# Moving one early input load to a second DMA queue in a transformer-block kernel

## The chip, the cores and the metric

The kernel runs on one core of one Trainium2 chip. The metric is the device time of one execution in microseconds (us). A profile comes from one further execution; its span (first to last instruction) is about 1.7 us shorter than that execution's time. All comparisons use runs classed as fast. A difference counts as "faster" or "slower" only beyond 2%.

## The reference

The input x has 2048 tokens of 640 numbers, in bf16. It is layer-normalised; then a linear-attention branch and a GELU branch are added to x.

```python
xn = layernorm(x)                                  # no learned scale
q, k, v = split(xn @ wqkv)                         # 32 heads of 20
phi = lambda t: where(t > 0, t + 1, exp(t)) + 1e-6
kv  = einsum("bhsd,bhse->bhde", phi(k), v)
z   = phi(k).sum(over s)
o   = (phi(q) @ kv) / (phi(q) @ z + 1e-6)
out = x + o @ wo + gelu(xn @ w1 + b1) @ w2 + b2
```

## The kernel before

The tokens come in 16 tiles of 128. "x0" to "x3" are the loads of tiles 0 to 3 (160 KB each). The K columns of wqkv come in two parts: part one is rows 0 to 383 (480 KB), part two the last 256 rows (320 KB). DMAs are issued from two queues: the sync queue and ScalarE's queue.

```python
def load_x(t0, t1, queue=nc.sync):
    queue.dma_start(out=x_all[:, t0:t1, :], in_=xv[:, t0:t1, :])

def load_wk(k0, k1):
    nc.scalar.dma_start(out=wqk[:, k0:k1, D : 2 * D], in_=wqkv_v[:, k0:k1, D : 2 * D])

load_x(0, 1)          # x0 .. x3, all on the sync queue
load_x(1, 2)
load_x(2, 3)
load_x(3, 4)
# ... later loads are issued further down
nc.vector.memset(eps_t[:], EPS)
nc.vector.memset(neg_half[:], -0.5)
nc.vector.memset(wqk[:, 0, D : D + TOK], 0.0)   # "gate": K part one must wait for it
load_wk(0, 3)         # K part one, ScalarE's queue
load_wk(3, NC)        # K part two
load_x(4, 8, nc.scalar)
```

The memset writes bytes that the K load overwrites, so the load may not be issued before it. It serves only to hold the load back. The compute that follows has this order; every engine keeps its own order of instructions:

```python
emit_warm(10)                       # TensorE: ten matmuls on constants
emit_stats(0); emit_center(0)       # VectorE: mean and variance of tile 0; tile 0 centred
emit_T_first(0, ...)                # TensorE transposes tile 0, ScalarE copies it out
emit_warm(1)
emit_stats(1)
emit_later_loads()                  # W1 and others, sync queue
emit_stats(2)
emit_rstd(0, 2)                     # ScalarE: 1/sqrt(var + eps)
emit_norm(1)                        # VectorE: tile 1 normalised
emit_Ka(0)                          # TensorE: K of tile 0, needs both K parts
emit_rstd(2, 3)
emit_T_first(1, ...)
emit_stats_half(3, 0)               # VectorE: first half of x3's statistics
emit_norm(2)                        # VectorE: tile 2 normalised, behind it
emit_stats_half(3, 1)
emit_Kb(0)                          # TensorE: the last 128 K columns of tile 0
emit_T(2, ...)                      # TensorE transposes tile 2
emit_Ka(1, 0, 3)
# ... K of tiles 1 to 3, then the GELU branch; TensorE is full from here on
```

Tile 2 is normalised behind an instruction that needs x3.

Of the kernel before, what the change touches and what calls it, by code (L numbers as in the profile page):

```python
# [15 lines left out]
def kernel(  # L16
# [12 lines left out]
    nc = tc.nc  # L29
# [4 lines left out]
    S, D = x2d.shape  # L34
# [6 lines left out]
    TOK = 512  # L41
# [34 lines left out]
    wqk = early.tile([P, NC, 2 * D], BF16, name="wqk", tag="early")  # L76
# [47 lines left out]
# [4 lines that stand above are left out]
        nc.scalar.dma_start(out=wqk[:, k0:k1, D : 2 * D], in_=wqkv_v[:, k0:k1, D : 2 * D])  # L128

    load_x(0, 1)  # L130
    load_x(1, 2)
    load_x(2, 3)
    load_x(3, 4)

# [8 lines left out]

    nc.vector.memset(eps_t[:], EPS)
    nc.vector.memset(neg_half[:], -0.5)
    nc.vector.memset(wqk[:, 0, D : D + TOK], 0.0)
    load_wk(0, 3)
    load_wk(3, NC)
    load_x(4, 8, nc.scalar)
# [1081 lines left out]
```

## Time and profile before

| | |
|---|---|
| time, median of the 20 runs beside the changed kernel | 197.07 us (196.64 to 197.34) |
| span in the trace | 195.4 us |
| TensorE busy | 188.8 us, 97% |
| TensorE's waits after its start | 1.2 + 0.4 + 0.2 us, all before 9.6 us |
| transpose of tile 2 | 9.60 us |

These lines are from the page of the kernel before: busy time by engine, the granted TensorE clock in tenths over 40 slices, and the chain that ended last, by engine. In all such lines PE is TensorE (PEld its weight loads), DVE is VectorE, ACT is ScalarE, POOL is GpSimd and SP the sync engine; a q after the name means that the engine's queue is issuing. L and a number is a line of the kernel.

```profile
...
PE 188.8 (97%) x1229; PEld 111.3 (57%) x1240; DVE 163.8 (84%) x393; ACT 89.8 (46%) x165; POOL 21.4 (11%) x54
...
PEclk9999999999999999999999999999999999999999
...
PE 93%; DMA 3%; issue 1%; DVE 1%; SPq 1%
...
```

TensorE bounds the kernel: it is busy 97% of the span at full clock (the mean granted clock is 1.0; a 9 stands for 90% or more), and 93% of the last chain is TensorE. A change elsewhere can help only where TensorE waits. The list of TensorE's waits (who waited, for whom, us in total, times, longest) of the kernel before:

```profile
...
PE bank_198 L242 <- DVE xn L229: 1.2, 1, 1.2
...
PE bank_170 L318 <- DMA wqk<-in_A_wqkv_dram: 0.4, 1, 0.4
PE bank_170 L318 <- ACT xnT L268: 0.2, 1, 0.2
```

L242 is the transpose of tile 2, L318 the K matmuls. Why is there a wait of 1.2 us for a VectorE result? The chain of waits over the first 12 us (start, duration, what):

```profile
...
2.19 6.48 DMA x_all<-in_A_x_dram
...
8.70 0.04 DVE stats L209
...
9.11 0.44 DVE xn L229
...
9.60 0.45 PE bank_198 L242 x5
...
```

After the issues on the sync queue (left out) comes one piece of 6.48 us: x3 travelling until 8.67 us. Then VectorE starts x3's first statistics half, normalises tile 2 at 9.11, and TensorE can transpose it at 9.60. The timeline of the same stretch (start, duration, engine, line, what; in brackets the idle time before it and what ended it) shows the issues and the landings:

```profile
...
0.81 1.82 SPq L125 DMA_DIRECT2D x_all<-in_A_x_dram  x4
...
0.99 0.27 DVE L146 MEMSET wqk<- 128x256 uint32 x1
...
1.29 0.96 ACTq L128 DMA_DIRECT2D wqk<-in_A_wqkv_dram  x2
...
3.13 0.89 DVE L209 BATCH_NORM_STATS2 stats<-x_all 128x6 f32<-128x320 bf16 x2 [1.87 <-DMA x_all<-in_A_x_dram]
...
6.13 0.89 DVE L209 BATCH_NORM_STATS2 stats<-x_all 128x6 f32<-128x320 bf16 x2 [0.40 <-DMA x_all<-in_A_x_dram]
...
8.70 0.50 DVE L209 BATCH_NORM_STATS2 stats<-x_all 128x6 f32<-128x320 bf16 x1 [1.12 <-DMA x_all<-in_A_x_dram]
...
```

The four x issues take 1.82 us, about 0.45 us each. The memset ends at 1.26 us and ScalarE issues K part one at 1.29. VectorE starts on x0 at 3.13, on x2 at 6.13 and on x3 at 8.70 us. The DMA view from 4.1 to 4.6 us (packets, MB, share of the 16 DMA engines' time; q1 is the sync queue, q10 ScalarE's) shows why x2 and x3 are late:

```profile
...
q10 hardware_dynamic: 153, 0.20, 106.0%
q1 hardware_dynamic: 1, 0.00, 0.1%
...
```

ScalarE's queue moves 153 packets of K part one, the sync queue a single packet, although x2 was issued at 1.72 us. The trace's records of landings give the order x0 3.11, x1 4.50, K part one 5.60, x2 6.11, K part two 7.06, x3 8.67 us. This is the order of issue over both queues. But x3 came 1.6 us after K part two, and its 160 KB need only some 0.4 us (an estimate, at the 390 GB/s seen from 4 to 5 us). The view from 7 to 8 us shows what slowed it:

```profile
...
q10 hardware_dynamic: 73, 0.37, 91.4%
q1 hardware_dynamic: 44, 0.04, 12.2%
...
```

ScalarE's queue was by then on x4 to x7 (640 KB, issued at 2.28 us, 0.1 us after x3). Its packets are of 5 KB and those of x3 of 1.3 KB, so x3 got 0.04 MB of that microsecond and x4 to x7 0.37. Behind K part two alone x3 would have landed near 7.5 us by the same estimate, and VectorE was free for it at 7.58. So by this estimate the load of x4 to x7 is part of the cause of the wait for x3. This is argued, not shown: no run held that load back alone.

The Trainium skill's page "DMA: Bandwidth & Descriptors", section "Queues, rings and completion order", says that each DMA engine takes turns between the queues that have work, packet by packet. Between 4.1 and 4.6 us this trace does not show such turns. Whether x2 already lay before the engines at 4.1 us is not shown.

### The profile page before, as it was taken

How to read it: one execution, taken by the hardware profiler on the slowest of the kernel's cores; microseconds unless marked ns; L12 is line 12 of the kernel's file. 1: busy time of each engine (PE TensorE's matmuls, PEld its weight loads, DVE VectorE, ACT ScalarE, POOL GpSimd, SP SyncE). 2: the span in 40 equal slices, each digit the busy share in tenths (PEclk: the TensorE clock that was granted, in tenths of full speed). 3: DMA queues.
4: the chain of work that ended last, by engine and by line, in shares of the span. 5: the costliest groups of instructions: out<-in, count | busy, mean ns of one | idle time of the engine just before them, and what ended most of it. 6: DMA issues, size and time to landing. Idle time of an engine off the chain costs nothing.

```text
span 195.4 us, 3334 instructions
## 1 busy us (share of the span) xinstructions
PE 188.8 (97%) x1229; PEld 111.3 (57%) x1240; DVE 163.8 (84%) x393; ACT 89.8 (46%) x165; POOL 21.4 (11%) x54
## 2 busy tenths in 40 slices
PE   8699999999999999999999999999999999999993
PEld 2364444544445454444445777767767777777772
DVE  4678988999699999597787999989999999777442
ACT  2459676559579678899795230050011010110100
POOL 1004071003219200001500100000000000000000
PEclk9999999999999999999999999999999999999999
DMA  5999446944144000000008875400201021010112
GB/s 173 388 285 393 176 91 140 352 150 89 38 151 105 0 0 2 0 0 3 0 0 205 307 240 164 129 3 2 70 0 60 7 70 47 22 67 3 67 56 78
DMA packets 24447, 20.19 MB, mean 103 GB/s; under 512 B 11120, under 2 KB 24048, under 8 KB 24432
## 3 DMA queue, kind: packets, MB, share of 16 engines
q1 hardware_dynamic: 23472, 18.36, 30.8%
q10 hardware_dynamic: 960, 1.64, 2.3%
q8 instruction: 9, 0.15, 0.3%
q14 instruction: 6, 0.05, 0.1%
HBM read 12.78 MB, written 5.24 MB: 92 GB/s over the span
## 4 chain that ended last, share of the span: by engine, by line
PE 93%; DMA 3%; issue 1%; DVE 1%; SPq 1%
DMA x_all<-in_A_x_dram 3%; PE bank_1274 L832 2%; PE bank_1283 L832 2%; PE bank_1210 L803 2%; PE bank_1557 L975 1%; PE bank_2113 L975 1%; PE bank_1435 L975 1%; PE bank_1945 L975 1%; PE bank_2029 L975 1%; PE bank_1861 L975 1%; PE bank_1772 L975 1%; PE bank_1683 L975 1%; PE bank_1399 L832 1%; PE bank_1387 L832 1%; PE bank_1511 L975 1%; PE bank_1581 L975 1%
## 5 line engine op out<-in xcount | busy, mean ns | idle before, releaser
L975 PEld LDWEIGHTS <-xn 128*128 128x128 f16 x198 | 19.0, 98 | 7.2
L493 PEld LDWEIGHTS <-w_91 128*128 128x128 bf16 x120 | 11.7, 98 | 13.9
L209 DVE BATCH_NORM_STATS2 stats<-x_all 128x6 f32<-128x320 bf16 x32 | 13.8, 469 | 3.4 <-DMA x_all<-in_A_x_dram 3.4
L481 PEld LDWEIGHTS <-wqk 128*128 128x128 bf16 x100 | 9.6, 98 | 11.1
L318 PEld LDWEIGHTS <-xnT 128*128 128x128 bf16 x80 | 7.2, 98 | 7.3 <-issue 0.7
L832 PEld LDWEIGHTS <-xn 128*128 128x128 bf16 (+1 forms) x80 | 7.8, 98 | 3.0
L229 DVE TENSOR_SCALAR xn<-x_all,mv,rstd 128x640 bf16<-128x640 bf16 x16 | 6.2, 436 | 3.7 <-POOL rstd L225 3.6
L890 DVE TENSOR_TENSOR pqT<-pqT,xnT 128x256 bf16<-128x256 bf16 (+1 forms) x30 | 8.5, 328 | 0.0
L636 PEld LDWEIGHTS <-w_91 128*128 128x128 bf16 (+1 forms) x48 | 4.6, 98 | 5.6 <-issue 0.3
L328 PEld LDWEIGHTS <-xnT 128*128 128x128 bf16 x80 | 5.8, 98 | 3.5
L990 PEld LDWEIGHTS <-Sq 128*128 128x128 f16 x66 | 6.3, 98 | 2.5 <-DVE Sq L881 0.2
L420 DVE TENSOR_TENSOR x_all<-x_all,b2b 128x640 bf16<-128x640 bf16 x16 | 7.0, 479 | 0.0
L172 POOL TENSOR_SCALAR_AFFINE_SELECT emask<-emask 128x160 int8<-128x160 int8 (+3 forms) x20 | 6.7, 346 | 0.9
L279 DVE TENSOR_SCALAR pqT<-pqT 128x512 bf16<-128x512 bf16 x20 | 5.7, 285 | 0.6 <-ACT pqT L276 0.6
L990 PEld LDWEIGHTS <-pqT 128*128 128x128 bf16 x50 | 4.8, 98 | 1.8
L975 PEld LDWEIGHTS <-hT_80 128*128 128x128 bf16 x48 | 4.7, 98 | 1.7
L975 PEld LDWEIGHTS <-hT_79 128*128 128x128 bf16 x48 | 4.7, 98 | 1.8
L1067 ACT CAST late<-bank_1487 128x320 bf16<-128x320 f32 x1 | 0.4, 425 | 10.4 <-PE bank_1490 L1063 10.4
L198 PE MATMUL bank_125<-const-bfloat16-1.0 128*128 128x512 bf16 x10 | 4.3, 615 | 0.8 <-PEq L1215 0.8
L881 DVE TENSOR_TENSOR Sq<-pqT 128x256 f16<-128x256 bf16 x16 | 4.2, 280 | 0.0
L735 DVE TENSOR_TENSOR pk<-pk,GT 128x512 bf16<-128x512 bf16 x10 | 4.2, 420 | 0.0
L636 PEld LDWEIGHTS <-wv 128*128 128x128 f16 x24 | 2.3, 97 | 3.2 <-issue 0.7
(648 smaller groups left out, 508.9 us busy)
## 6 DMA issues: line engine op xcount, KB each, us to landing
xnT<-rec_rows SPq DMA_DIRECT2D x20, 128.0 KB, 2.9
out_dram<-late SPq DMA_DIRECT2D x14, 160.0 KB, 1.8
w_91<-in_B_w_dram SPq DMA_DIRECT2D x2, 960.0 KB, 7.4
w_93<-in_B_w_dram SPq DMA_DIRECT2D x3, 640.0 KB, 7.6
x_all<-in_A_x_dram SPq DMA_DIRECT2D x2, 640.0 KB, 9.6
wqk<-in_A_wqkv_dram SPq DMA_DIRECT2D x1, 800.0 KB, 8.0
wv<-in_A_wqkv_dram SPq DMA_DIRECT2D x1, 800.0 KB, 6.2
woA<-in_A_wo_dram SPq DMA_DIRECT2D x5, 160.0 KB, 3.6
```

The costliest lines, as they stand in the source:

```text
L172: nc.gpsimd.affine_select(out=out, in_=out, compare_op=ALU.is_ge, fill=0.0, base=base, pattern=pattern, channel_multiplier=sign)
L209: nc.vector.bn_stats(out=st[:, half, :], in_=x_all[:, t, half * HALF : (half + 1) * HALF])
L229: nc.vector.tensor_scalar(out=xn[:, t, ds], in0=x_all[:, t, ds], scalar1=mv[:, t, 0:1], scalar2=rstd[:, t : t + 1], op0=ALU.subtract, op1= ...
L318: nc.tensor.matmul(K_ps[t][:], lhsT=xnT[:, k, t * P : (t + 1) * P], rhs=wqk[:, k, D : D + TOK], start=(k == 0), stop=(k == NC - 1),)
L420: nc.vector.tensor_tensor(out=x_all[:, t, :], in0=x_all[:, t, :], in1=b2b[:], op=ALU.add)
L481: nc.tensor.matmul(ps[:], lhsT=wqk[:, k, m * P : (m + 1) * P], rhs=xnT[:, k, gs], start=(k == 0), stop=(k == NC - 1),)
L493: nc.tensor.matmul(ps[:], lhsT=w1[:, k, j * P : (j + 1) * P], rhs=xnT[:, k, g * TOK : (g + 1) * TOK], start=(k == 0), stop=(k == NC - 1),)
L636: nc.tensor.matmul(self.ps[name][:], lhsT=left[:, c, js], rhs=x_block(*block, c) if block else Tx({4: 3, 5: 0, 6: 1, 7: 2}[p], c), start=( ...
L832: nc.tensor.matmul(ps if len(right.shape) == 3 else ps.rearrange("p (c n) -> p c n", c=NC), lhsT=left[:, t, self.i], rhs=right[:, t], star ...
L890: nc.vector.tensor_tensor(out=pqT[:, c, gs], in0=pqT[:, c, gs], in1=xnT[:, c, gs], op=ALU.mult)
L975: nc.tensor.matmul(self.ps[name][:, cols], lhsT=left[:, j], rhs=right[:, j, cols], start=(start and j == 0), stop=False, skip_group_check= ...
L990: nc.tensor.matmul(self.ps[name][:, cols], lhsT=left[:, c], rhs=right[:, c, cols], start=False, stop=(stop and c == CH - 1), skip_group_ch ...
```

## The change

The intent: issue x1 on ScalarE's queue, ahead of the K parts, so that x2 and x3 move up by one slot on the sync queue. x1 now holds the K parts back, so the memset goes.

```diff
     load_x(0, 1)
-    load_x(1, 2)
+    load_x(1, 2, nc.scalar)
     load_x(2, 3)
     load_x(3, 4)
     ...
     nc.vector.memset(eps_t[:], EPS)
     nc.vector.memset(neg_half[:], -0.5)
-    nc.vector.memset(wqk[:, 0, D : D + TOK], 0.0)
     load_wk(0, 3)
```

## The prediction

> **What bounds the kernel now.** TensorE: 97% busy over the 195.4 us span, at granted clock 1.0 (page, parts 1 and 2), and 93% of the chain that ended last. The wait list gives TensorE three waits after its start: 1.2 us for xn (L229, before the transpose of tile 2), 0.4 us for the second K-weight part, 0.2 us for a ScalarE copy, all before 9.6 us. The chain of waits, from the start: the four x issues on the sync queue (0.81, 1.25, 1.72, 2.15 us), x3's transfer from 2.19 to 8.67 us (6.48 us, the longest piece), xn of tile 2 at 9.11 to 9.55, the transpose at 9.60, and from there TensorE only. So all that this change can buy is the 1.23 us hole before 9.60 us, plus perhaps part of the 0.42.
>
> **Why x3 is late.** VectorE's program puts x3's first statistics half ahead of xn of tile 2, so tile 2 waits for x3, the sixth of seven transfers issued. The DMA view shows that the queues do not simply share: from 4.1 to 4.6 us the ScalarE queue moved 153 packets (first K part) and the sync queue 1, though x2 had been issued at 1.72. Transfers move nearly in the order of issue, over both queues. That agrees with the Trainium skill ("DMA: Bandwidth & Descriptors", "Issuing engines are not separate DMA queues"): both run on the same 16 DMA engines.
>
> **What changes.** Removed: a 0.27 us VectorE memset, which held ScalarE's first K issue to 1.29 us. Moved: x1 to the ScalarE queue. An issue takes about 0.45 us, so ScalarE issues x1 at about 0.8 and the K parts at 1.3 and 1.75, nearly unmoved. The sync queue issues x2 at 1.25 and x3 at 1.7, one slot earlier. That small time changes the order: x2 can pass the first K part (480 KB, 1.2 us at the 390 GB/s seen) and x3 the second (320 KB, 0.8 us). Bytes are unchanged. I expect x2 in at 4.6 to 5.5 us (was 6.1), x3 at 6 to 7 (was 8.7), the second K part near 7.1 as before.
>
> **Cost.** x0 and x1 are now issued together; x0 may land up to 0.5 us later than its 3.13 us.
>
> **Critical path.** VectorE then runs without waits from x0's landing: statistics 0, centring, statistics 1 and 2, xn 1, half of statistics 3, xn 2, about 5.1 us by the timeline's durations, ending near 8.25 us plus x0's delay. TensorE needs K part two (7.1), then 0.59 of matmul, transpose 1 and tile 0's rest columns, until 8.4. The transpose of tile 2 starts at 8.4 to 8.9 instead of 9.60: a gain of 0.7 to 1.2 us. Later dependencies have slack: the first W1 half lands near 12 us (needed near 13.3), group 1's last transposed piece near 31.6 (needed near 32.6). So the gain should reach the end.
>
> **Predicted: 196.3 us**, 195.7 to 197.0 eight times in ten. Chances: faster by over 2% 0.01, within 2% 0.98, slower by over 2% 0.01.
>
> **Signs.** Right: VectorE no longer waits for x2 or x3; TensorE's 1.2 us wait for xn falls under 0.5; transpose of tile 2 at 8.4 to 8.9. Wrong: x0 past 3.6 us, x3 past 7.3, the K part past 7.5, or the 1.2 us back as a TensorE wait before 35 us.
>
> **What would make it wrong.** If ScalarE's issue goes first, x1 delays x0 by a whole transfer and 0.5 to 1 us of the gain goes. If K part one goes ahead of x2, x2 and x3 gain little. If x0 and x1 together fill the slow start of 2.5 to 3.5 us (182 to 205 GB/s), K part two comes early and the gain reaches 1.4.

## The result

The changed kernel took 196.32 us (median of 10 runs, 196.06 to 197.35), the kernel before 197.07 us (median of 20). The ratio is 0.9974, with a 95% interval of 0.9961 to 0.9987: within 2%, but clear of no change. Ratios here are the mean time of one kernel's fast runs over that of the other's in the same rounds, so they are not quite the ratio of the medians. The difference shows here: the mean gain is 0.5 us and the median gain 0.75, because four of the ten runs lay at 196.7 to 197.35 us. The trace, from a run of 196.20 us, has a span of 194.5 us, 0.9 less than before.

The page of the changed kernel, busy time by engine and the last chain by engine:

```profile
...
PE 188.7 (97%) x1229; PEld 111.2 (57%) x1240; DVE 163.3 (84%) x392; ACT 89.8 (46%) x165; POOL 22.1 (11%) x54
...
PE 94%; DVE 2%; DMA 2%; issue 1%
...
```

TensorE works as long as before (188.7 us). The DMA share of the chain falls from 3% to 2% of the span (x0's 3.1 us stand where x3's 6.5 us stood), and the VectorE share rises from 1% to 2%, so only part of what DMA lost is gained. TensorE's waits in the changed kernel (L263 is the transpose of tiles 0 and 1, L317 the K matmuls; its start-up wait is left out):

```profile
...
PE bank_140 L263 <- DVE xn L234: 0.6, 1, 0.6
PE bank_169 L317 <- ACT xnT L267: 0.2, 1, 0.2
PE bank_177 L263 <- DVE xn L228: 0.2, 1, 0.2
```

The 1.2 us wait for the norm of tile 2 and the 0.4 us wait for K part two are gone. In their place TensorE waits 0.6 us at its first transpose, for tile 0, and 0.2 us for the norm of tile 1. That is 1.8 us of waits before and 1.0 after, about the gain in span. The chain of waits of the changed kernel in the first 12 us:

```profile
...
0.81 3.11 DMA x_all<-in_A_x_dram
...
8.40 0.28 PE bank_191 L327 x5
...
8.69 0.45 PE bank_197 L241 x5
...
```

The chain now begins with x0 (0.81 to 3.92 us) instead of x3. The VectorE and TensorE steps between are left out. The timeline shows the new issues and the dates on VectorE and TensorE:

```profile
...
0.80 0.39 ACTq L125 DMA_DIRECT2D x_all<-in_A_x_dram  x1
...
0.81 1.35 SPq L125 DMA_DIRECT2D x_all<-in_A_x_dram  x3
...
1.22 1.02 ACTq L128 DMA_DIRECT2D wqk<-in_A_wqkv_dram  x2
...
3.94 0.89 DVE L208 BATCH_NORM_STATS2 stats<-x_all 128x6 f32<-128x320 bf16 x2 [2.97 <-DMA x_all<-in_A_x_dram]
...
8.21 0.43 DVE L228 TENSOR_SCALAR xn<-x_all,mv,rstd 128x640 bf16<-128x640 bf16 x1
...
8.69 0.45 PE L241 MATMUL bank_197<-identity,xn 128*128 128x128 bf16 x5
...
```

The first line is x1 on ScalarE's queue, the second x0, x2 and x3 on the sync queue. K part one is issued at 1.22 us (before: 1.29), so it has hardly moved. VectorE has no bracket with a wait for x2 or x3 any more. It starts on x0 0.81 us later than before, normalises tile 2 at 8.21 (done at 8.64), and the transpose of tile 2 starts at 8.69 us, 0.91 us earlier. TensorE is busy with tile 0's last columns until 8.67, so the norm and TensorE are ready at nearly the same time. The landings, from the trace's records: x0 3.92, x1 4.11, x2 4.44, K part one 5.76, x3 6.20, K part two 7.10 us. So x2 passed K part one, and x3 passed K part two. Both were near ties: the issue of x2 began at 1.25 us, 0.03 us after that of K part one, and those of x3 and K part two began 0.01 us apart (1.72 and 1.73). Under e4 stands a trace with the same loads in which they shared the engines instead. x3 is now also issued 0.55 us before x4 to x7 (1.72 and 2.27). The DMA view from 2.5 to 3.4 us shows what became of x0:

```profile
...
q1 hardware_dynamic: 135, 0.16, 50.3%
q10 hardware_dynamic: 129, 0.15, 47.4%
...
```

x0 is on the sync queue (q1) and x1 on ScalarE's (q10), issued 0.01 us apart, and the two queues share the engines almost packet for packet, 135 to 129. These equal counts fit the turns of the skill's page; they do not show how long one turn is. The same view of the kernel before has 140 packets on q1 and 5 on q10 in this stretch.

### The profile page after: what moved, and what is told of

Its sections match the earlier page's. It is cut to its first block, busy times and chain, and to the rows that moved or that the text cites. A ratio compares the mean times of both kernels' runs of the same rounds, so it can differ in the third digit from the quotient of the medians.

```text
span 194.5 us, 3333 instructions
## 1 busy us (share of the span) xinstructions
PE 188.7 (97%) x1229; PEld 111.2 (57%) x1240; DVE 163.3 (84%) x392; ACT 89.8 (46%) x165; POOL 22.1 (11%) x54
## 4 chain that ended last, share of the span: by engine, by line
PE 94%; DVE 2%; DMA 2%; issue 1%
PE bank_1273 L831 2%; PE bank_1282 L831 2%; PE bank_1209 L802 2%; DMA x_all<-in_A_x_dram 2%; PE bank_1771 L974 1%; PE bank_1556 L974 1%; PE bank_1434 L974 1%; PE bank_2112 L974 1%; PE bank_2028 L974 1%; PE bank_1944 L974 1%; PE bank_1860 L974 1%; PE bank_1682 L974 1%; DVE stats L208 1%; PE bank_1386 L831 1%; PE bank_1398 L831 1%; PE bank_1510 L974 1%
## 5 line engine op out<-in xcount | busy, mean ns | idle before, releaser
L317 PEld LDWEIGHTS <-xnT 128*128 128x128 bf16 x80 | 7.2, 98 | 6.7 <-ACT xnT L267 0.6
```

What stands on the lines that cost most here:

```text
L317: nc.tensor.matmul(K_ps[t][:], lhsT=xnT[:, k, t * P : (t + 1) * P], rhs=wqk[:, k, D : D + TOK], start=(k == 0), stop=(k == NC - 1),)
```

## The experiments

The table shows, for each trace, when VectorE starts on x0, when tile 2's transpose starts, and the span. The kernels "before" and "after" lead.

| trace | x0 used | transpose of tile 2 | span | its time |
|---|---|---|---|---|
| before | 3.13 | 9.60 | 195.4 | 197.09 |
| after | 3.94 | 8.69 | 194.5 | 196.20 |
| after, again | 3.99 | 8.75 | 194.5 | 196.22 |
| e1: x1 moved, gate kept | 4.15 | 9.31 | 195.7 | 197.48 |
| e2: gate removed only | 3.69 | 10.21 | 196.0 | 197.72 |
| e3: before, norm of tile 2 first | 3.22 | 8.48 | 194.4 | 196.09 |
| e3, again | 3.15 | 8.41 | 194.3 | 196.09 |
| e4: after, norm of tile 2 first | 4.03 | 8.78 | 194.6 | 196.27 |
| e5: after, x1 held | 3.08 | 10.73 | 197.1 | 198.86 |
| e5, again | 3.17 | 9.12 | 195.0 | 196.68 |
| e7: K parts after all x | 3.13 | 9.59 | 195.5 | 197.32 |

In all of them but e1 and e5's first trace, the span moves with the date of tile 2's transpose to within 0.15 us: what is won or lost before 10 us reaches the end.

My theory was that x3's wait in front of tile 2's norm is what the change takes away, and that x0 beside x1 is what it pays. The rivals were that the freed K weights pay (e1, e2), that the loads as such pay (e3), and that x0 was late by chance (e5).

### e1: x1 moved, gate kept

```diff
-    load_x(1, 2)
+    load_x(1, 2, nc.scalar)
```

> Only half of the change: x1 goes to ScalarE's queue, the memset that holds the K weights stays (it ends near 1.26 us, when ScalarE has just finished issuing x1). Theory (the order of issue of the x tiles is what pays; the gate costs nothing once x1 stands before it): same picture as the whole change. First K part issued at 1.22 to 1.30 us, VectorE's wait for x0 ends at 3.7 to 4.1 us, no wait for x2 or x3, transpose of tile 2 near 8.7 us, time within 0.2 us of the changed kernel, ratio to before 0.995 to 0.998. Rival (the freed K weights pay): no gain, ratio 0.999 to 1.001.

The ratio is 0.9966 (0.9947 to 0.9985), the median 196.26 us. So moving x1 alone gives the whole gain, and the memset costs nothing once x1 stands before it (K part one at 1.29 us). The traced execution itself was the odd one of six: 197.48 us against 196.16 to 196.49. Its dates for x0 (4.15) and tile 2 (9.31) therefore missed my expectation, but it shows what a late execution of this order looks like. From its chain of waits up to 37 us:

```profile
...
1.73 6.56 DMA wqk<-in_A_wqkv_dram
...
20.16 5.73 DMA xn_rows<-xn
...
31.12 2.92 DMA xnT<-xn_rows
...
```

K part two arrives at 8.29 us instead of 7.10. The records of landings show that 14 of its 16 completions had come by 7.07 us, the 15th came at 7.49 and the last at 8.29: one DMA engine was 1.2 us behind. The skill's page "DMA: Bandwidth & Descriptors", section "Why a DMA increments its semaphore by 16 and not by 1", says that a DMA runs on up to 16 engines that finish independently and is complete only at the full count; this is a case of it. The same execution lost time a second time. Its stores of normalised rows (the second line) landed at 25.9 us, the transposed loads that follow them at 34.03, and TensorE, which wanted the last piece about 33.5 us, stood still again (the third line). Matched matmul by matmul, the trace is 0.2 us ahead of the kernel before until 33 us and 0.36 us behind it after that. In the good trace of the changed kernel the last of these pieces lands at 31.84 us and is needed at 32.8; before it was 31.62 and 33.7. So the slack there shrank from 2.1 to about 1 us, because TensorE came earlier and the stores did not (the last one landed at 23.62 us before and 23.85 after).

### e2: gate removed only

```diff
-    nc.vector.memset(wqk[:, 0, D : D + TOK], 0.0)
```

> The other half: the memset goes, x1 stays on the sync queue. Theory: the first K part is then issued at 0.80 us together with x0 and the second at about 1.25, so both stand before or beside x1 in the order of issue; x0 shares the engines with the K part and lands at 3.7 to 4.1 us instead of 3.13, x1 lands after 5.3 us, x3 still not before 7.5 us. TensorE's wait for K part two vanishes, but VectorE waits for x1 and the transpose of tile 2 starts at 9.6 us or later: ratio 1.000 to 1.006. Rival (the freed K weights pay): ratio 0.995 to 0.998.

The ratio is 1.0063 (1.0033 to 1.0092): slower, just above my range. The rival is refuted. The timeline:

```profile
...
0.80 1.00 ACTq L128 DMA_DIRECT2D wqk<-in_A_wqkv_dram  x2
...
3.69 0.89 DVE L208 BATCH_NORM_STATS2 stats<-x_all 128x6 f32<-128x320 bf16 x2 [2.72 <-DMA x_all<-in_A_x_dram]
...
7.96 0.89 DVE L208 BATCH_NORM_STATS2 stats<-x_all 128x6 f32<-128x320 bf16 x2 [1.33 <-DMA x_all<-in_A_x_dram]
...
10.21 0.45 PE L241 MATMUL bank<-identity,xn 128*128 128x128 bf16 x5
...
```

K part one is issued at 0.80 us, together with x0. x0 is used 0.56 us later than in the kernel before, x2 only at 7.96 us, and the transpose of tile 2 starts at 10.21. The memset was doing useful work: it kept the K parts behind x0 and x1. TensorE's wait for K part two did vanish, and it was worth nothing, since the norms were later.

### e3: the kernel before, with two VectorE instructions exchanged

```diff
-    emit_stats_half(3, 0)
     emit_norm(2)
+    emit_stats_half(3, 0)
```

> No load is touched: the kernel before, with two neighbouring VectorE instructions exchanged, so that tile 2 is normalised before the first statistics half of tile 3. Theory (x3's late landing is paid only because tile 2's norm stands behind the wait for x3): x3 still lands near 8.7 us, but the norm of tile 2 runs at about 7.9 us, its transpose starts at 8.3 to 8.5 us instead of 9.60, and TensorE runs on from there; gain 1.0 to 1.3 us, ratio 0.9935 to 0.995, more than the change itself, since x0 is not delayed. Rival (the gain of the change comes from the loads as such): no gain, or the hole moves to the transpose of tile 3; ratio 0.998 to 1.001.

No load is touched. The ratio is 0.9952 (0.9940 to 0.9964), the median 196.09 us. The timeline:

```profile
...
7.98 0.45 DVE L229 TENSOR_SCALAR xn<-x_all,mv,rstd 128x640 bf16<-128x640 bf16 x1 [0.29 <-ACT rstd L220]
...
8.48 0.45 PE L242 MATMUL bank<-identity,xn 128*128 128x128 bf16 x5
8.66 0.89 DVE L209 BATCH_NORM_STATS2 stats<-x_all 128x6 f32<-128x320 bf16 x2 [0.24 <-DMA x_all<-in_A_x_dram]
...
```

x3 is still late (VectorE starts on it at 8.66 us), but tile 2 no longer waits for it: norm at 7.98, transpose at 8.48 us. The whole gain of the change is had without moving a load. That the late x3 hurt only through VectorE's order is shown.

### e5: x1 held on ScalarE's queue

```diff
-    load_x(1, 2, nc.scalar)
     load_x(2, 3)
     load_x(3, 4)
     ...
+    nc.vector.memset(x_all[:, 1, 0:TOK], 0.0)
+    load_x(1, 2, nc.scalar)
     load_wk(0, 3)
```

> The changed kernel, with x1's issue on ScalarE held by a memset into x1's own tile (as the K weights were held before), so that x0 is issued alone and x1 beside x2; the K parts are issued one slot later, at about 1.7 and 2.15 us. Theory (the changed kernel gave back part of its gain because x0 and x1 share the engines packet by packet): x0 lands at 3.1 to 3.3 us as before instead of 3.92, x3 still before 7.3 us, the transpose of tile 2 at 8.2 to 8.5 us, ratio 0.9935 to 0.996, 0.2 to 0.5 us better than the change. Rival (x0 is late for another reason, such as a slow start of that execution): x0 stays near 3.9 us and there is no gain over the change.

This was half a miss. x0 is back at 3.08 us, so x0's delay in the changed kernel does come from x1 being issued beside it. But there is no gain: ratio 1.001 (0.9978 to 1.0042). I had thought that the K parts could come one slot later at little cost. The views by stretch of the traced execution (columns: stretch, its length, then busy us and instruction count of PE, PEld, DVE, ACT and POOL; then granted clock, DMA share, GB/s):

```profile
...
6.00:7.00 1.00, 0.00 (x0) 0.10 (x1) 0.96 (x4) 0.90 (x4) 0.00 (x0) 1.00 1.08 389
7.00:8.00 1.00, 0.00 (x0) 0.00 (x0) 0.90 (x3) 0.25 (x2) 0.00 (x0) 1.00 1.11 418
8.00:9.00 1.00, 0.98 (x4) 0.39 (x4) 0.72 (x3) 0.00 (x0) 0.00 (x0) 0.81 0.96 236
9.00:10.00 1.00, 1.00 (x6) 0.48 (x5) 0.00 (x0) 0.00 (x0) 0.00 (x0) 0.50 0.86 295
...
11.00:12.00 1.00, 1.00 (x7) 0.56 (x5) 0.50 (x3) 0.95 (x3) 0.00 (x0) 0.50 1.01 221
12.00:13.00 1.00, 1.00 (x9) 0.57 (x8) 0.77 (x3) 0.00 (x0) 0.00 (x0) 0.98 1.08 163
...
```

TensorE stood still for 2.2 us, up to 8.02 us, waiting for K part one. Its granted clock was 1.0 until 8.62 us and 0.50 from there to 12.04 (the 0.81 is a mean over both), so the matmuls took about twice as long. Two late engines made this execution worse (14 of K part one's 16 completions by 6.41 us, the last at 7.98). The skill's page "TensorE: Matmul & The Clock Gate", Part 1, says that an idle array falls to half clock after an idle window of about 3.4 us and needs as much sustained work to come back. The trace agrees on the half clock and on the length (0.50 for 3.41 us). But here a wait of 2.2 us was enough: in the 3.41 us before the fall TensorE had worked for 1.2 us. To see an ordinary execution I looked again:

> One more look at the changed kernel with x1 held. Its first traced execution ran at 198.86 us with K part one usable only at 8.02 us, a TensorE wait of 2.2 us and a granted clock of 0.50 from 9 to 12 us, while the other five executions of that label took 196.5 to 198.1. If that was one bad execution: x0 again at 3.1 us, K part one before 6.5, K part two 7.2 to 7.8 (one issue slot, 0.45 us, later than in the changed kernel), clock 1.0 throughout, transpose of tile 2 at 8.7 to 9.2 us, time 196.5 to 197.0. If the later K issue is itself the cause: K part one again after 7.5 us.

```profile
...
3.17 0.89 DVE L209 BATCH_NORM_STATS2 stats<-x_all 128x6 f32<-128x320 bf16 x2 [1.92 <-DMA x_all<-in_A_x_dram]
...
7.29 1.43 PE L318 MATMUL bank<-wqk,xnT 128*128 128x512 bf16 x5 [1.15 <-DMA wqk<-in_A_wqkv_dram]
...
9.12 0.44 PE L242 MATMUL bank<-identity,xn 128*128 128x128 bf16 x5
...
```

x0 is early again and the clock is 1.0 throughout, but TensorE can start its K matmuls only at 7.29 us, after a wait of 1.2 us, and transposes tile 2 at 9.12. K part one landed at 7.25 us, K part two at 8.09: my "before 6.5" and "7.2 to 7.8" were wrong, and "after 7.5" was not reached either. So this order of the loads is itself a cause, bad execution or not: it cost more than it saved on x0. The issue slot does not explain all of it. K part one was issued 0.48 us later than in the changed kernel and landed 1.5 us later. From 3.75 to 4.75 us DMA moved 253 GB/s here and 277 in e5's first trace, against 396 in the changed kernel. Why is not shown.

### e7: K parts after all four x tiles

```diff
-    nc.vector.memset(wqk[:, 0, D : D + TOK], 0.0)
+    nc.vector.memset(wqk[:, 0:3, D : 2 * D], 0.0)
```

> The kernel before, all four x tiles on the sync queue, with the memset that holds the K weights made larger (three chunks of columns), so that the K parts are issued only after x3. No x tile moves to another queue. Theory (transfers are served in the order of issue over both queues; what the change bought is x2 and x3 ahead of the K parts, what it paid is x0 beside x1): x0 at 3.1 us, no VectorE wait for x2, none or under 0.3 us for x3, in exchange K part one 0.5 to 1 us later than 5.6 and part two at 7.4 to 8.3 us; transpose of tile 2 at 8.5 to 9.3 us, ratio 0.9945 to 0.999. Rival (queues share evenly, so it takes two queues to bring x3 early): x3 as late as before, transpose of tile 2 at 9.5 us or later, ratio 1.000 or more.

The larger memset holds the K parts until 2.02 us. The timeline:

```profile
...
2.02 1.00 ACTq L128 DMA_DIRECT2D wqk<-in_A_wqkv_dram  x2
...
7.75 1.45 PE L318 MATMUL bank<-wqk,xnT 128*128 128x512 bf16 x5 [1.71 <-DMA wqk<-in_A_wqkv_dram]
...
9.59 0.44 PE L242 MATMUL bank<-identity,xn 128*128 128x128 bf16 x5
...
```

VectorE starts on x0 at 3.13 us and never waits for another tile, with all four on one queue: x2 landed at 5.50 us and x3 at 6.99 (before: 6.11 and 8.67). So it does not take two queues to bring x3 early, as the rival said; issuing the K parts later does it. Sharing itself is not refuted. From 4.0 to 5.25 us the queues moved 115 and 146 packets, though x2 had been issued 0.3 us before K part one, and x3 landed 0.7 us before K part one (7.71), though issued 0.17 us after it. So the order of issue is a rough guide only. The dates of the K parts, of the transpose and the ratio all missed my expectation, and the last two lie where the rival put them, but through the K parts: the K matmuls start at 7.75 us, after a TensorE wait of 1.7 us, and the ratio is 1.0081 (1.0045 to 1.0117), beyond my range. The traced execution took 197.32 us, no more than the kernel before. The mean is pulled up by four runs of 198.3 to 200.0 us whose mean granted clocks were 0.982 to 0.991; the other two, at 197.2 and 197.3, had 0.997 and 1.000. I read this as the half-clock stretch of e5 again (e5's first trace, with one such stretch, has a mean of 0.989), but those four have no trace.

### e4: both cures

```diff
     # in the changed kernel
-    emit_stats_half(3, 0)
     emit_norm(2)
+    emit_stats_half(3, 0)
```

> Both cures together: the changed loads and the exchanged VectorE instructions. Theory (both remove the same wait, for x3): they do not add up. In the changed kernel the norm of tile 2 is no longer held by x3 but by its own rstd at 8.14 us and TensorE is busy with tile 0's columns until 8.67, so the transpose of tile 2 moves by less than 0.1 us and the median stays within 0.15 us of the changed kernel. Rival (two separate gains): a further 0.5 us or more, median under 195.8 us.

```profile
...
8.78 0.45 PE L241 MATMUL bank<-identity,xn 128*128 128x128 bf16 x5
...
```

The transpose of tile 2 (above, from the timeline) does not move against the changed kernel, and the median is 196.36 us beside 196.22. The two cures remove the same wait and do not add up. The loads of this trace are those of the changed kernel, issued within 0.03 us of the same dates, yet x2 landed at 5.57 us and x3 at 7.03 (changed kernel: 4.44 and 6.20). From 3.75 to 4.75 us the queues moved 119 and 200 packets side by side. VectorE waited for neither tile, so this cost nothing. One of six runs took 198.65 us, at a mean clock of 0.989, which pulls the ratio to 0.9986 (0.9950 to 1.0022).

### The changed kernel and e3 again, for their spread

> The changed kernel once more, for its spread. Of its first ten timed runs seven lay at 196.1 to 196.4 us, three at 196.7 or above and two of those at 197.3, while 31 runs of the kernel before all lay between 196.64 and 197.34. The one execution of this kind that has a trace (the first half of the change alone, 197.48 us) had one of the 16 DMA engines about 1.2 us behind, so that TensorE waited 0.8 us for the second K part and again near 33 us. If that belongs to the new order of the loads: one to three of these runs again at 196.7 or above, none of the kernel before above 197.5, median 196.2 to 196.4. Rival (the spread came from the chip of that hour): all runs within 0.4 us of each other.

> The kernel before with the two VectorE instructions exchanged, beside the changed kernel on one chip. If the old order of the loads has no late K part: all runs within 0.4 us, median 196.0 to 196.2, so 0.1 to 0.3 us under the changed kernel's median and 0.3 to 0.6 under its mean. Rival (any kernel without the wait for x3 shows the late runs, because that wait hid them): one to three runs at 196.7 or above here too.

(The text on record miscounts the first ten runs: six lay under 196.4 us and four at 196.7 or above.) Neither expectation came true, except the changed kernel's median of 196.22 us: it had no run at 196.7 or above, and e3's runs spread over 0.7 us. e3's rival did come true, with one run at 196.78. The changed kernel's five runs lay between 196.05 and 196.51 us (ratio 0.9958, 0.9946 to 0.9970). e3's lay between 196.09 and 196.78 (0.9963, 0.9951 to 0.9975). On this chip the two are equal, and neither kernel is shown to beat the other. Over all, 6 of the 27 timed executions with the changed loads and a prompt x1 (after, e1, e4) were at 196.7 us or above, and 1 of the 10 of e3. These counts are too small to say that the order of the loads makes the late executions. All 53 runs of the kernel before lay between 196.64 and 197.35 us.

## Why the prediction was right, and where it was not

The time (196.3 predicted, 196.32 measured) and the mechanism were right. Point by point:

- **The hole.** The 1.2 us wait of TensorE for tile 2 was the main thing to win. e3 shows this without the loads: taking away this wait gives 1.0 us of span.
- **The order of issue.** x2 was predicted in at 4.6 to 5.5 us and came at 4.44, x3 at 6 to 7 and came at 6.20, K part two near 7.1 and came at 7.10. e7 shows that no second queue is needed for it. Here there was luck: x2 and x3 won near ties against the K parts in three of the four traces that have these loads, and in e4's they had to share the engines. "Order of issue" also left out x4 to x7, beside which x3 crawled in the kernel before (7 to 8 us); x3 gained, it seems, by getting clear of them too.
- **The memset.** Said to be replaced by x1. e1 and e2 show both halves of this.
- **The cost on x0 was mis-sized.** "Up to 0.5 us later" was 0.81 us, and the prediction's own sign "x0 past 3.6 us" came true. I had reckoned with one of two effects. x0 shares with x1 from 2.5 us on, which accounts for some 0.4 us by an estimate: the time of another 160 KB at the 390 GB/s seen. The other is a slower start. Up to 2.5 us the DMA view counts 95 packets in the kernel before and 30 in the changed one. Over all eleven traces it counts 95 to 116 where x0 is issued alone (before, e3, e5, e7) and 30 to 64 where a second queue issues at the same moment (after, e1, e2, e4). Why two issues at once start more slowly is not shown.
- **The VectorE chain was mis-sized the other way.** The prediction had 5.1 us from x0 to the end of tile 2's norm. It took 4.70 us (3.94 to 8.64). The two errors partly cancel: 8.64 against a predicted 8.25 to 8.75, and the transpose at 8.69 inside the predicted 8.4 to 8.9. That the median is right to 0.02 us is luck.
- **"Later dependencies have slack"** held in the good trace, and the 0.91 us at tile 2 arrives as 0.9 us of span. It did not hold in e1's late execution, where group 1's transposed rows cost another 0.57 us. The slack had been stated from dates of which only TensorE's moves.
- **The spread was not foreseen.** Four of ten runs gave back 0.4 us or more, so the mean gain is 0.5 us. One such execution, in e1, is traced: one slow DMA engine. In the second trace of the changed kernel K part two was 0.5 us late too (7.60), with a TensorE wait of 0.3 us, and that cost nothing (196.22 us). Why that engine was slow, and whether the new order makes this more frequent, stays open. It is argued, not shown, that the kernel before hides a late K part two, because TensorE had to wait for x3 afterwards in any case.

## What to carry to other kernels

Before moving a load to another queue, look at which instruction of the consuming engine stands in front of the one that matters: exchanging two instructions (e3) gave the same gain as reordering the loads, with no price on x0. When loads are reordered, rank them by the date at which each is needed: every slot given to one is taken from another (e2, e5 and e7 each moved some loads forward and lost on others). Look also at what is issued just behind the load that matters, on the other queue. And a long wait of TensorE can be paid once more in granted clock: it was after the 2.2 us of e5's first trace, and not after 1.7 us in e7's or 1.9 us in e2's.

## What the Trainium skill lacked or had wrong

- "DMA: Bandwidth & Descriptors", "Queues, rings and completion order", tells of turns packet by packet between queues. The runs show nearly equal counts for transfers issued together (135 to 129 packets, issued 0.01 us apart). But a transfer issued 0.43 us after another queue's 480 KB transfer got 1 packet to its 153 in the half microsecond looked at. No page says when a later transfer of another queue has to stand back like this.
- The same page says, in "Issuing engines are not separate DMA queues", that issuing from several engines at once saves only issue time, which is usually small beside the transfer. Here an issue slot of 0.45 us moved a landing by 1.7 us (x2: 6.11 to 4.44) and 2.5 us (x3: 8.67 to 6.20).
- No page tells that two queues issuing their first load at the same moment start more slowly than one: 30 to 64 packets moved by 2.5 us in five traces, against 95 to 116 in six with one issue.
- No page gives the spread between the 16 DMA engines of one load: for K part two there are 1.7 us between its first completion and its last in e1 (6.58 and 8.29 us), against 0.3 us in the changed kernel's trace and 1.0 us in its second one.
- "TensorE: Matmul & The Clock Gate", Part 1, has the clock fall after an idle window of about 3.4 us. In e5 a wait of 2.2 us, in a stretch of 3.41 us of which TensorE worked 1.2, was followed by a granted clock of 0.50 until 12.04 us.
